# Attention scores as row tiles with each head on its own partition half, part of layer 2's output weights decoded inside layer 2, and a new order of work

## The chip, the cores and the metric

The kernel runs on one core of one Trainium2 chip. The metric is the device time of one execution in microseconds. Before the change three runs took 1127.84, 1130.23 and 1132.29 us; the median is 1130.23 us.

## The reference

The program is an attention layer followed by two dense layers. Inputs and results are float32.

```python
# attention: q, k, v are (4, 8, 576, 64); q and k get a rotary embedding first
scores = 1/sqrt(64) * q_rot @ k_rot.T          # per batch and head, 576 x 576
attn   = exp(scores - rowmax);  attn /= rowsum + 1e-9
x      = attn @ v                              # laid out as (2304, 512)
# layer 1: w_in (512, 2048), w_out (2048, 512)
h = x @ w_in;   g = h * clip(h + 3, 0, 6) / 6;   x = g @ w_out
# layer 2: same sizes, a has 4 coefficients and b has 2
h = x @ w_in
P = a0 + a1*h + a2*h^2 + a3*h^3
Q = 1 + |b0|*|h| + |b1|*h^2
out = (P / (Q + 1e-6)) @ w_out
```

The weights reach the core as 64-bit floats, so each weight has to be turned into float32 on the core ("decoded").

## The kernel before

**Precision.** Most products are split in two: a float32 number is scaled and written as a float16 head plus a float16 remainder ("hi" and "lo"), and a product is the sum hi*hi + hi*lo + lo*hi, accumulated in PSUM. Layer 2's second product uses a float32 form of matmul with the same three terms.

**Attention.** The work goes by pairs of heads: 4 batches with 4 pairs each. For one pair, `start_qk` (line 898) loads k and q into a tile `nat`. The 576 rows of a head lie as four groups of 128 rows and a tail of 64; the two heads share the fifth group, so the tile has NB = 9 groups of 128 rows for two heads. ScalarE takes a bound of the magnitudes (`bound`, line 749), a small matmul with ones adds it over the partitions (`total`, line 758), and VectorE makes a power-of-two scale of it (`pow2`, line 695). `prep_qk` (line 919) applies the rotation on VectorE (lines 934, 941, 944), writes hi (line 629, 631 or 635 by engine) and lo (line 954), side by side in 128 columns, and one DMA transpose on SyncE's queue brings them to `qkt`, in which the partitions are 64 hi dimensions and 64 lo dimensions. Two more transfers (line 964) write `k2`, the same keys with the two partition halves swapped.

`unit` (line 968) is one block of scores. A "full" unit has 128 query rows of each of the two heads (2 x 576 scores a row); a "small" unit has the tails, 64 rows of each head on the two halves of the output partitions. Every score is two matmuls over all 128 partitions (line 1002): one with `qkt` (hi*hi + lo*lo) and one with `k2` (hi*lo + lo*hi). There are 64 full units and 16 small ones. VectorE takes the row maximum (line 1006), ScalarE the exponential (line 1018), the result is split in hi and lo (lines 629 or 633, and 1026), transposed by DMA (line 1029, `pt`), multiplied with v on TensorE (line 1057), evicted (`xu`) and normalised (`norm`), and transposed by DMA again into `xt` (line 1097), which lies in the attention pool.

**Layer 1.** `layer1` (line 1123) takes 256 tokens at a time; nine blocks in all. For 16 slices of the hidden dimension it does the first product (line 1152), the activation on ScalarE and VectorE (lines 1159, 1161, 1165), then the second product (line 1181) and the write of the result to memory (`y1d`, line 1193). A ninth block collects the tails of the four batches.

**Weights.** `load_raw` (line 717) loads one 512 KB tile of 64-bit weights; `decode` (line 726) turns it into float32 with two ScalarE passes (lines 734, a Prelu, and 736) and one VectorE pass (line 739). Layer 1's 32 tiles are used from on-chip memory. For layer 2, `prep_w2` (line 822) decodes 32 tiles (16 of W_in, then 16 of W_out) while attention and layer 1 run and writes each to memory (`w2d`, line 828); in layer 2, `split_w2` (line 1296) reads them back through three buffers `w2s` (line 1298) and splits them.

**Layer 2.** Five blocks of 512 tokens (the last has 256), 16 steps each. A step is a first product (line 1380), thirteen passes on ScalarE and VectorE (lines 1388 to 1404) and a second product accumulated over the steps (line 1413). Layer 2's tiles lie in two pools: `p2` takes the space of the attention pool and opens when every operation on the attention pool is done (`to_left`, line 1265), `p2r` takes the space of layer 1.

**The order.** Nothing is issued where it stands in the code. `op` records each operation with the engines that may do it, its cost, its priority and its data dependencies, and `order` (line 452) walks through a model of the engines in time: whenever an engine is free it takes the ready operation with the smallest priority number. The result is a fixed order of instructions for each engine and queue. The priorities come from the position in the program (`at`, `at2`) plus offsets by tile name (`o_...`, and `z_...` for the first batch) in the table `PR`. A string such as `'AG'` in the table names the engines that may do an operation (A ScalarE, D VectorE, G GpSimd), the first one preferred; `pen` is added to the priority on the others. Nearly all transfers are issued by SyncE's queue, in order; a transfer that has to wait for a buffer or for data holds up those behind it.

Of the kernel before, what the change touches and what calls it, by code (L numbers as in the profile page):

```python
# [10 lines left out]
F32 = mybir.dt.float32  # L11
# [12 lines left out]
S = 576  # L24
D = 64
HP = 4
NB = 9
DM = 512
# [10 lines left out]
 'c01': 7.051,  # L39
 'e': 2,  # L40
 'e_ev': 'AD',
 'e_ev0': 'DA',
 'e_gh': 'G',
 'e_gh0': 'AD',
# [4 lines left out]
 'e_mx': 'AG',  # L49
 'e_mx0': 'A',  # L50
 'e_ob': 'A',
 'e_qk': 'AGD',
 'e_qk0': 'A',
# [6 lines left out]
 'e_v': 'GD',  # L60
 'e_v0': 'DA',
# [11 lines left out]
 'e_y': 'D',  # L73
# [6 lines left out]
 'l0q': 111.276,  # L80
 'l1o': 10.002,
 'l1p': -1.281,
 'l1r': 77.612,
 'lead': 12.176,
 'lead0': -2.288,
# [4 lines left out]
 'o_': -4.68,  # L90
 'o_ab': -119.56,
 'o_ac0': -215.72,
 'o_ac1': -584.53,
 'o_ac2': -339.1,
 'o_ac3': -294.85,
 'o_acc': -425.76,
 'o_bb': 473.96,
 'o_cf': 224.73,
 'o_d': 309.78,
 'o_down': -26.62,  # L100
 'o_downi': -228.51,
 'o_dv': 109.2,
 'o_e': -286.55,
 'o_f32': 34.2,
 'o_g2l': 57.65,
 'o_gh': 370.8,
 'o_gl': -30.13,
 'o_h': 2.51,
 'o_h2': -146.66,
 'o_half': -517.61,  # L110
 'o_hh': 10.41,
 'o_hr': -514.06,
 'o_hs': -4.18,
 'o_hx': 11.06,
 'o_ident': -545.53,
 'o_k2': 25.35,
 'o_lgh': 105.85,
 'o_lgl': -50.66,
 'o_lq': 85.0,
 'o_lr': -318.72,  # L120
 'o_ls': 103.57,
 'o_lt': -33.88,
 'o_mx': 10.42,
 'o_na': -356.99,
 'o_nat': 12.98,
 'o_ob': -14.69,
 'o_ones': -646.58,
 'o_p1': 325.81,
 'o_p16': 10.73,
 'o_p16h': 293.66,  # L130
 'o_p16l': -306.11,
 'o_pt': -5.34,
 'o_pth': -589.79,
 'o_ptl': 669.69,
 'o_pw': 229.41,
 'o_pwi': -37.76,
 'o_qal': -278.91,
 'o_qam': -211.74,
 'o_qb': -353.38,
 'o_qk16': 1213.36,  # L140
 'o_qkt': -39.84,
 'o_qpi': -16.04,
 'o_qps': 13.14,
 'o_qpv': -190.27,
 'o_r': 15.85,
 'o_r0': 729.05,
 'o_raw': 45.94,
 'o_ropea': 11.43,
 'o_ropeb': -325.11,
 'o_s': 8.48,  # L150
 'o_shift': 92.35,
 'o_so': 597.84,
 'o_t': -774.55,
 'o_t0': 231.84,
 'o_t1': 745.61,
 'o_tab': -1032.75,
 'o_u': -155.38,
 'o_v9': 22.39,
 'o_vam': -425.01,
 'o_vm4': -590.92,  # L160
 'o_vnat': 254.14,
 'o_vnat0': 5.77,
 'o_vnat1': -226.94,
 'o_vpi': -611.24,
 'o_vps': -339.75,
 'o_vpv': 145.01,
 'o_vqi': 128.34,
 'o_vqs': -100.16,
 'o_vqv': 238.1,
 'o_vv': -599.43,  # L170
 'o_w0_': -195.86,
 'o_w1_': -207.38,
 'o_w2_': 89.43,
# [45 lines left out]
 'q_w2s': 'Q',  # L219
# [102 lines left out]
 'z_vps': 988.81,
# [1197 lines left out]
```

## Time and profile before

| | before |
|---|---|
| median of three runs | 1130.23 us |
| profiled execution, its own time | 1126.76 us |
| its span, first to last instruction | 1125.0 us |
| TensorE busy | 978.0 us (87%) |
| VectorE busy | 923.3 us (82%) |
| ScalarE busy | 783.8 us (70%) |
| GpSimd busy | 100.3 us (9%) |
| moved by DMA | 142.28 MB |

Busy times are sums over the instructions of an engine. In the rows PE is TensorE, PEld its weight loads, DVE VectorE, ACT ScalarE, POOL GpSimd, SP SyncE; a "q" behind a name is the engine's queue. L1002 is line 1002 of the kernel. A matmul's bar includes the time it takes to drain, so bars of consecutive matmuls overlap, and the distance between their starts tells what each one occupies. An "idle" entry names what ended the wait.

### The profile page before, as it was taken

The numbers are of one execution on the slowest core, as the hardware profiler recorded it, in microseconds if no ns is written. First come the engines' busy times: TensorE is split into PE (matmuls) and PEld (weight loads), VectorE is DVE, ScalarE is ACT, GpSimd is POOL, SyncE is SP. The second block draws the span as 40 slices with busy tenths as digits, with TensorE's granted clock in tenths as the row PEclk, the third lists the DMA queues.
The fourth block names the chain that finished last, engine by engine and source line by source line (L and its number), as shares of the span: only waits on it lengthen the run. The fifth ranks groups of instructions, "written<-read, shape, count | busy, mean of one in ns | idle before, by whom it ended". The sixth has DMA issues, their size and how long they took to land.

```text
span 1125.0 us, 20071 instructions
## 1 busy us (share of the span) xinstructions
PE 978.0 (87%) x7702; PEld 733.6 (65%) x7702; DVE 923.3 (82%) x1571; ACT 783.8 (70%) x1401; POOL 100.3 (9%) x124
## 2 busy tenths in 40 slices
PE   1344588889889899999899999799999999999996
PEld 1223377777778778788788888466566566556674
DVE  4999989899888898889883525799898898898886
ACT  7878977687665666656763327778786776686785
POOL 0200021001122011401020100000000000000000
PEclk9975789999999999999999999999999999999999
DMA  7989994998999879897997324412010010010010
GB/s 244 244 203 238 235 205 110 197 177 166 207 195 175 165 144 201 174 219 166 205 193 163 129 95 137 135 50 59 33 38 1 20 38 1 1 38 1 1 38 20
DMA packets 280081, 142.28 MB, mean 126 GB/s; under 512 B 239664, under 2 KB 257072, under 8 KB 279984
## 3 DMA queue, kind: packets, MB, share of 16 engines
q1 hardware_dynamic: 277040, 135.72, 54.0%
q10 hardware_dynamic: 2944, 5.28, 2.0%
q8 instruction: 60, 0.98, 0.4%
q14 instruction: 37, 0.30, 0.1%
HBM read 61.26 MB, written 17.83 MB: 70 GB/s over the span
## 4 chain that ended last, share of the span: by engine, by line
DVE 27%; PE 22%; ACT 20%; DMA 14%; issue 6%; SPq 1%; POOL 0%; ACTq 0%; DVEq 0%
PE h L1152 8%; DMA pt<-p 8%; PE h L1181 7%; DVE lt L1394 3%; ACT lr L1397 3%; ACT ls L1389 3%; ACT lq L1388 3%; PE h L1057 3%; DVE lq L1392 2%; DVE lq L1399 2%; DVE lt L1402 2%; ACT lt L1390 2%; ACT lr L1398 2%; DVE lt L1395 2%; DVE lt L1400 2%
## 5 line engine op out<-in xcount | busy, mean ns | idle before, releaser
L1152 PE MATMUL h<-xt,w 128*128 128x256 f16 x1728 | 200.4, 276 | 5.9 <-ACT xu L629 2.2
L1413 PE MATMUL ac<-w,lgh 128*128 128x512 f32 x576 | 188.9, 409 | 6.5 <-ACT ob L629 4.2
L1152 PEld LDWEIGHTS <-w 128*128 128x128 f16 x1728 | 169.5, 99 | 28.6 <-issue 7.2
L1181 PE MATMUL h<-gh,w 128*128 128x256 f16 x1080 | 187.9, 273 | 0.0
L1181 PEld LDWEIGHTS <-w 128*128 128x128 f16 x1620 | 157.0, 98 | 17.9
L1380 PEld LDWEIGHTS <-w 128*128 128x128 f16 x960 | 90.1, 98 | 102.8 <-issue 20.8
L1181 PE MATMUL h<-gl,w 128*128 128x256 f16 x540 | 147.2, 273 | 0.0
L1413 PEld LDWEIGHTS ac<-w,lgh 128*128 128x128 f32 x576 | 106.2, 188 | 36.4 <-ACT lgh L1403 6.8
L1018 ACT ACTIVATE e<-s,mx,qal 128x576 f32<-128x576 f32 (+1 forms) x144 | 113.4, 832 | 23.7 <-DVE p L1026 11.4
L1413 PE MATMUL ac<-w,lgl 128*128 128x512 f32 x288 | 115.6, 401 | 2.6 <-DVE lgl L1404 1.9
L1057 PE MATMUL h<-v,pt 128*128 128x130 f16 (+3 forms) x1600 | 90.0, 214 | 31.9 <-DMA pt<-p 18.9
L1380 PE MATMUL hh<-x,w 128*128 128x512 f16 (+1 forms) x516 | 109.3, 363 | 4.7 <-ACT ls L1389 4.7
L1026 DVE TENSOR_TENSOR p<-e,p 128x1152 f16<-128x1152 f32 (+1 forms) x80 | 100.9, 1263 | 12.7 <-ACT p L629 11.9
L1057 PEld LDWEIGHTS <-pt 128*128 128x128 f16 (+1 forms) x1600 | 84.6, 104 | 39.6 <-DMA pt<-p 24.7
L1002 PEld LDWEIGHTS <-qkt 128*128 128x128 f16 (+1 forms) x704 | 52.6, 110 | 80.3 <-issue 41.2
L1006 DVE TENSOR_REDUCE mx<-s 128x2 f32<-128x1152 f32 (+1 forms) x80 | 98.8, 1241 | 0.5 <-PE s L1002 0.5
L1002 PE MATMUL s<-qkt 128*128 128x512 f16 (+3 forms) x352 | 70.2, 305 | 31.0 <-ACT e L1018 17.7
L1159 ACT ACTIVATE t<-h,half,d 128x512 f32<-128x512 f32 (+1 forms) x96 | 61.5, 667 | 46.2 <-PE h L1152 36.1
L1380 PE MATMUL hx<-x,w 128*128 128x512 f16 (+1 forms) x444 | 91.9, 356 | 1.3 <-DVE t L635 1.3
L736 ACT ACTIVATE raw<-raw,down 128x512 int32<-128x512 uint16 x64 | 48.5, 760 | 39.8 <-DMA raw<-in_moe_w_out_dram 25.7
L1400 DVE SCALAR_TENSOR_TENSOR lt<-lt,na,lr 128x512 f32<-128x512 f32 (+1 forms) x80 | 55.3, 694 | 18.5 <-ACT lr L1398 18.3
L1413 PEld LDWEIGHTS ac<-w,lgl 128*128 128x128 f32 x288 | 54.0, 188 | 24.3 <-DVE lgl L1404 13.4
(155 smaller groups left out, 1651.7 us busy)
## 6 DMA issues: line engine op xcount, KB each, us to landing
raw<-in_moe_w_in_dram SPq DMA_DIRECT2D x32, 512.0 KB, 4.9
raw<-in_moe_w_out_dram SPq DMA_DIRECT2D x32, 512.0 KB, 4.3
w2d<-f SPq DMA_DIRECT2D x32, 256.0 KB, 4.8
w2s<-w2d SPq DMA_DIRECT2D x32, 256.0 KB, 2.6
y1d<-t SPq DMA_DIRECT2D x18, 256.0 KB, 2.7
vnat<-in_v_dram SPq DMA_DIRECT2D x16, 256.0 KB, 3.4
nat<-in_k_dram SPq DMA_DIRECT2D x16, 256.0 KB, 4.0
nat<-in_q_dram SPq DMA_DIRECT2D x16, 256.0 KB, 3.4
```

The source lines that it names most:

```text
L736: op("A", c_act(512, 1) + 40, lambda e: act.activation(t()[:, :, 0], t().rearrange("p n two -> p (n two)").bitcast(U16).rearrange("p (n x) ...
L1002: pe.matmul(x[i][0], lhsT=x[i][1], rhs=x[i][2], start=(x[i][3] == 0), stop=(x[i][3] == 1))
L1006: op("D", c_dve(n), lambda e: vec.reduce_max(mx()[:, 0, 0:g], sv().rearrange("p (g n) -> p g n", g=g), axis=AX.X, negate=True), r=[s], w=[ ...
L1018: op("A", c_act(n // g, 2, False), lambda e, h=h: act.activation(et()[:, h * (n // g):(h + 1) * (n // g)], sv()[:, h * (n // g):(h + 1) * ...
L1026: op(EN("lo"), c_sub(n), lambda e: EL[e].tensor_tensor(ph()[:, n:2 * n], et()[:, 0:n], ph()[:, 0:n], ALU.subtract), r=es + [(ph, 0)], w=[( ...
L1057: pe.matmul(ob()[r0:r0 + m, o:o + k], lhsT=w, rhs=vv[:, 0:k], start=(z == 0 and j == 0), stop=(z == 1 and j == 4))
L1152: pe.matmul(hp()[:, o:o + NQ], lhsT=wt[kk]()[:, z, c:c + 128], rhs=x, start=(n == 0), stop=(n == 11))
L1159: act.activation(seg(t, c, n), seg(hp, c, n), AF.Relu, bias=half(), scale=x()[:, g:g + 1])
L1181: pe.matmul(yp()[:, o:o + NQ], lhsT=w[:, s_, m_ * 128:(m_ + 1) * 128], rhs=gt()[:, f], start=(f == 0 and z == 0), stop=(f == KF - 1 and z ...
L1380: pe.matmul(hp()[:, 0:n], lhsT=wi[kk]()[:, z, c:c + 128], rhs=xt()[:, kk, y, 0:n], start=(i == 0), stop=(i == 11))
L1400: op("D", l2_dve(n, 1), lambda e: vec.scalar_tensor_tensor(s(t), s(t), na()[:, 0:1], s(rr), ALU.add, ALU.mult), r=[rr, na], w=[t])
L1413: pe.matmul(accs[j][i]()[0:m], lhsT=gt()[:, x:x + m], rhs=wt(), start=(f == 0 and z == 0), stop=(f == KF - 1 and z == 2))
```

## The change

Keys and queries get the same layout as the values already have: `nat` becomes two standing tiles with five groups of 128 rows for each head (NS = 5), whose fifth group is zero on the other head's half of the partitions (zeroed once). The rotation works on 1280 instead of 1152 elements a partition, its last step is written to a new tile `rot` in two instructions, with the two heads side by side, and hi and lo become separate planes. After the transpose (20 blocks of 128 x 128 instead of 18) each head lies on its own half of the partitions, 64 dimensions each. The copy `k2` and its transfers go. A score is now three matmuls, hi*hi + hi*lo + lo*hi; in a full unit, head 0's are over partitions 0 to 63 and head 1's over 64 to 127, into different banks of PSUM, and the tail's keys of both heads are one full-height matmul, since the zeros separate the heads. A small unit uses full-height matmuls throughout.

Fifteen of the 16 tiles of layer 2's W_out are no longer decoded in `prep_w2`; `load_w2` loads and decodes them in layer 2 into tiles of their own in the pool `p2`, and `split_w2` takes them from there. The buffers `w2s` go from three to two.

The table `PR` gets new values nearly throughout: priorities, offsets and engine choices. The planner's costs of transfers go up by some 10%.

```diff
+ NS = 5
- 'e_ev': 'AD', 'e_mx': 'AG', 'e_qk': 'AGD', 'e_v': 'GD', 'e_y': 'D', 'q_w2s': 'Q', 'pen': -1.576
+ 'e_ev': 'A',  'e_mx': 'DA', 'e_qk': 'GD',  'e_v': 'G',  'e_y': 'AD', 'q_w2s': 'QA', 'pen': -82.267
...
+    ntt = [tl("attn", [128, 2, 2, NS, D], F32, f"nat{i}") for i in range(2)]
+    for i in range(2):
+        for h in range(2):
+            op("D", 155, lambda e, i=i, h=h: vec.memset(ntt[i]()[64 - 64 * h:128 - 64 * h, :, h, 4], 0.0), w=[(ntt[i], "0")])
...
-        op(en, cost, lambda e: EL[e].tensor_tensor(t(), t(), tb(), ALU.add), r=[(tb, 0), (tb, 1)], w=[(nat, 0), (nat, 1)])
+        rot = tl("attn", [128, 2, NS, 2, D], F32, "rot", 1)
+        for i in range(2):
+            op(en, {"D": c_dve(640), "G": c_pool(640)}, lambda e, i=i: EL[e].tensor_tensor(
+                rot()[:, i].rearrange("p j h d -> p h j d"), nat()[:, i], tb()[:, 2 * i:2 * i + 2], ALU.add),
+               r=[nat, (tb, 0), (tb, 1)], w=[(rot, i)])
...
-        for h in range(2):
-            op(PR["q_k2"], c_in(490, 730, 250, 1850), lambda e, h=h: DE[e].dma_start(
-                out=k2()[64 * h:64 * h + 64], in_=r()[64 - 64 * h:128 - 64 * h, 0]), r=[(r, 0)], w=[(k2, h)])
...
         def mm(e):
+            def kq(i, z, r0, r1):
+                return qk()[r0:r1, i, z].rearrange("p j e -> p (j e)")
+            if both:
+                todo = [[(h, a, b, c, x) for x in ((0, 0), (0, 1), (1, 0))]
+                        for h, a, b, c in ((0, 0, 512, 0), (1, 640, 1024, 0), (1, 1024, 1152, 384))]
+                for h, a, b, c, (y, z) in [x for u in zip(todo[0], todo[1]) for x in u] + todo[2]:
+                    pe.matmul(s()[:, a:b], lhsT=kq(1, y, 64 * h, 64 * h + 64)[:, cc * 128:cc * 128 + 128],
+                              rhs=kq(0, z, 64 * h, 64 * h + 64)[:, c:c + b - a], start=(y + z == 0), stop=(y == 1))
+                for y, z in ((0, 0), (0, 1), (1, 0)):
+                    pe.matmul(s()[:, 512:640], lhsT=kq(1, y, 0, 128)[:, cc * 128:cc * 128 + 128],
+                              rhs=kq(0, z, 0, 128)[:, 512:640], start=(y + z == 0), stop=(y == 1))
+            else:
+                for y, z in ((0, 0), (0, 1), (1, 0)):
+                    pe.matmul(s()[:, 0:512], lhsT=kq(1, y, 0, 128)[:, 512:640], rhs=kq(0, z, 0, 128)[:, 0:512],
+                              start=(y + z == 0), stop=(y == 1))
+                for i, (y, z, h) in enumerate([(y, z, h) for y, z in ((0, 0), (0, 1), (1, 0)) for h in range(2)]):
+                    kk = kq(0, z, 0, 128)[:, 512 + 64 * h:576 + 64 * h].unsqueeze(1).to_broadcast([128, 2, 64])
+                    pe.matmul(s()[:, 512:640], lhsT=kq(1, y, 0, 128)[:, 512:640], rhs=kk, start=i == 0, stop=i == 5)
...
-    for z in range(2 * KF):
+    for z in range(2 * KF - PR["wd"]):
         at(PR["w20"] + z * (PR["w21"] - PR["w20"]) / (2 * KF))
         prep_w2(z // KF, z % KF)
...
+    def load_w2(f):
+        raw = load_raw(w2o, False, f, True)
+        w2f[1, f] = tl("p2", [128, 512], F32, f"w2f{f}")
+        decode(raw, w2f[1, f])
...
-        t = tl("p2", [128, 512], F32, "w2s", 3)
+        if (wi, f) in w2f:
+            t = w2f[wi, f]
+        else:
+            t = tl("p2", [128, 512], F32, "w2s", 2)
...
+    for f in range(KF - PR["wd"], KF):
+        at2(PR["wd0"] + PR["wd1"] * f)
+        load_w2(f)
```

## Rows read from the trace of the kernel before

**Rows 1.** Busy time by stage (start:end us, length, busy us and instructions, clock, DMA)

```profile
0.00:150.00 150.00, 62.29 (x443) 42.81 (x444) 124.19 (x235) 123.82 (x246) 15.89 (x20) 0.81 0.93 231
150.00:605.00 455.00, 417.50 (x4516) 351.99 (x4514) 396.44 (x631) 304.10 (x510) 74.08 (x88) 0.98 0.91 180
605.00:697.00 92.00, 91.16 (x837) 81.63 (x835) 37.52 (x67) 38.26 (x79) 10.29 (x16) 1.00 0.39 117
697.00:812.00 115.00, 108.02 (x510) 66.32 (x508) 100.66 (x166) 91.21 (x158) 0.00 (x0) 0.99 0.27 81
812.00:1125.00 313.00, 299.06 (x1406) 190.82 (x1404) 264.54 (x475) 226.44 (x410) 0.00 (x0) 1.00 0.05 18
```

**Rows 2.** Chain of waits from 150 to 605 us, its shares by line

```profile
by line: DMA pt<-p 16.1%; PE h L1152 10.7%; PE h L1181 9.6%; PE h L1057 6.2%; issue 5.8%; DMA raw<-in_moe_w_in_dram 4.6%; PE s L1002 4.3%; DVE mx L1006 3.7%; DVE p L1026 3.6%; DMA qkt<-ropea 3.1%; DVE gl L1165 2.6%; DVE t L1161 2.5%; DMA vn
```

**Rows 3.** TensorE's waits from 0 to 150 us: us in total, times, longest

```profile
PE h L1057 <- DMA pt<-p: 8.8, 6, 2.4
PE s L1002 <- DMA qkt<-ropea: 8.2, 2, 6.3
PE s L1002 <- DMA k<-qkt: 5.7, 3, 3.1
```

**Rows 4.** The same from 150 to 605 us

```profile
PE h L1057 <- DMA pt<-p: 10.1, 8, 2.1
```

**Rows 5.** Timeline of TensorE, one full unit: start us, us, instruction, [idle before]

```profile
267.38 0.57 PE L1002 MATMUL s<-qkt 128*128 128x512 f16 x2
...
268.36 0.27 PE L1181 MATMUL h<-gh,w 128*128 128x256 f16 x1
```

**Rows 6.** Timeline of TensorE, two small units one after the other

```profile
426.99 0.41 PE L1002 MATMUL s<-qkt 128*64 128x512 f16 x2
427.23 0.38 PE L1002 MATMUL s<-k,qkt 128*64 128x512 f16 x2
...
427.57 0.39 PE L1002 MATMUL s<-qkt 128*64 128x512 f16 x2
427.79 0.38 PE L1002 MATMUL s<-k,qkt 128*64 128x512 f16 x2
```

**Rows 7.** DMA queues (packets, MB, share of 16 engines), and the key copies' issues

```profile
q1 hardware_dynamic: 277040, 135.72, 54.0%
q10 hardware_dynamic: 2944, 5.28, 2.0%
...
k<-qkt ACTq DMA_DIRECT2D x26, 144.0 KB, 4.1
```

**Rows 8.** Groups by line and shape, VectorE: count, busy us, mean ns, idle before

```profile
L934 DVE SCALAR_TENSOR_TENSOR ropea<-nat,tab 128x576 f32<-128x576 f32 x32 | 24.0, 765 | 7.3 <-DMA qkt<-ropea 5.4 <-DMA k<-qkt 1.0 <-DMA nat<-in_q_dram 0.9
L941 DVE TENSOR_TENSOR nat<-nat,tab 128x1152 f32<-128x1152 f32 x16 | 21.6, 1350 | 0.2
...
L633 DVE COPY xu<-h 128x260 f32<-128x260 f32 x20 | 8.5, 424 | 3.9 <-PE h L1057 3.9
```

**Rows 9.** The same view, the decode of one weight tile

```profile
L736 ACT ACTIVATE raw<-raw,down 128x512 int32<-128x512 uint16 x64 | 48.5, 760 | 39.8 <-DMA raw<-in_moe_w_out_dram 25.7 <-DMA raw<-in_moe_w_in_dram 13.9
...
L739 DVE SCALAR_TENSOR_TENSOR f<-f,raw 128x512 int32<-128x512 int32 x33 | 23.0, 696 | 17.5 <-ACT f L734 17.4
L734 ACT ACTIVATE f<-raw 128x512 f32<-128x512 f32 x33 | 22.1, 670 | 9.3 <-DMA w2d<-f 9.3
```

**Rows 10.** Busy time by stage of line 734 alone, one pass per decoded tile

```profile
150.00:605.00 455.00, 16.14 (x24) 0.98 0.91 180
605.00:697.00 92.00, 5.31 (x8) 1.00 0.39 117
```

**Rows 11.** Timelines of SyncE's queue, TensorE and ScalarE at the start of layer 2

```profile
696.38 12.61 SPq L1298 DMA_DIRECT2D w2s<-w2d  x7
...
717.26 6.83 PE L1380 MATMUL hh<-x,w 128*128 128x512 f16 x24 [4.68 <-ACT ls L1389]
717.81 1.28 ACT L1397 ACT_TABLE_LOAD   x1
```

More of the change, by code (lines that the diff above doesn't have):

```diff
@@ new lines @@
+ 'o_half': -103.62,
+ 'o_hh': 15.68,
+ 'o_hr': -395.49,
+ 'o_hs': -5.71,
+ 'o_hx': 15.09,
+ 'o_ident': -403.8,
+ 'o_k2': -142.58,
+ 'o_lgh': 70.04,
+ 'o_lgl': -581.99,
+ 'o_lq': 18.14,
+ 'o_lr': -123.91,
+ 'o_ls': 304.83,
+ 'o_lt': -372.33,
+ 'o_mx': 15.84,
+ 'o_na': -465.11,
+ 'o_nat': -305.94,
+ 'o_nat0': 45.34,
+ 'o_nat1': 129.69,
+ 'o_ob': -15.17,
+ 'o_ones': -634.81,
+ 'o_p1': 895.42,
+ 'o_p16': 13.11,
+ 'o_p16h': 132.86,
+ 'o_p16l': -385.03,
+ 'o_pt': 34.12,
+ 'o_pth': -413.89,
+ 'o_ptl': 495.44,
@@ new lines @@
+ 'o_pw': 35.35,
+ 'o_pwi': -257.48,
+ 'o_qal': -687.9,
+ 'o_qam': -212.59,
+ 'o_qb': -803.88,
+ 'o_qk16': 825.26,
+ 'o_qkt': -454.57,
+ 'o_qpi': -159.44,
+ 'o_qps': -5.98,
+ 'o_qpv': -319.4,
+ 'o_r': 17.77,
+ 'o_r0': 473.98,
+ 'o_raw': 216.86,
+ 'o_raw2': -192.45,
+ 'o_ropea': 10.38,
+ 'o_ropeb': 132.9,
+ 'o_rot': -6.37,
+ 'o_s': 8.87,
+ 'o_shift': 88.64,
+ 'o_so': 281.85,
+ 'o_t': -1177.27,
+ 'o_t0': -37.55,
+ 'o_t1': 600.66,
+ 'o_tab': -1216.31,
+ 'o_u': -110.88,
+ 'o_v9': 213.87,
+ 'o_vam': 41.33,
@@ new lines @@
+ 'z_ac1': -643.66,
+ 'z_ac2': 1566.75,
+ 'z_ac3': 154.26,
+ 'z_acc': 1154.56,
+ 'z_bb': -548.32,
+ 'z_cf': 171.79,
+ 'z_d': 891.23,
+ 'z_down': 1027.25,
+ 'z_downi': -311.78,
+ 'z_dv': 582.63,
+ 'z_e': -131.84,
+ 'z_f32': -840.49,
+ 'z_g2h': 234.36,
+ 'z_gh': -385.88,
+ 'z_gl': -27.84,
+ 'z_h': -1.68,
+ 'z_h2': -499.0,
+ 'z_half': -882.07,
+ 'z_hh': 83.8,
+ 'z_hr': -325.04,
+ 'z_hs': -449.06,
+ 'z_hx': 187.72,
+ 'z_ident': -50.9,
+ 'z_k2': -456.94,
+ 'z_lgh': 352.19,
+ 'z_lgl': -1350.85,
+ 'z_lq': 587.76,
@@ new lines @@
+ 'z_lr': -382.08,
+ 'z_ls': 262.72,
+ 'z_lt': -543.66,
+ 'z_mx': 438.55,
+ 'z_na': -508.55,
+ 'z_nat': -151.59,
+ 'z_nat0': -464.6,
+ 'z_nat1': 11.97,
+ 'z_ob': -16.05,
+ 'z_ones': -370.9,
+ 'z_p1': 72.62,
+ 'z_p16': -106.48,
+ 'z_p16h': 49.47,
+ 'z_p16l': -1221.72,
+ 'z_pt': -181.03,
+ 'z_pth': 1132.41,
+ 'z_ptl': -260.59,
+ 'z_pw': -557.88,
+ 'z_pwi': -464.29,
+ 'z_qal': 147.31,
+ 'z_qam': -366.26,
+ 'z_qb': -448.13,
+ 'z_qk16': 808.95,
+ 'z_qkt': -233.39,
+ 'z_qpi': -201.97,
+ 'z_qps': 130.7,
@@ new lines @@
+ 'z_qpv': -620.02,
+ 'z_r': -548.83,
+ 'z_r0': -1018.46,
+ 'z_raw': -866.63,
+ 'z_raw2': 143.28,
+ 'z_ropea': -255.31,
+ 'z_rot': -353.19,
+ 'z_s': 1228.73,
+ 'z_shift': 350.91,
+ 'z_so': -201.04,
+ 'z_t': 423.53,
+ 'z_t0': -713.56,
+ 'z_t1': 161.79,
+ 'z_tab': -74.19,
+ 'z_u': 167.92,
+ 'z_v9': 490.1,
+ 'z_vam': 91.27,
+ 'z_vm4': 16.87,
+ 'z_vnat': -734.01,
+ 'z_vnat0': 366.59,
+ 'z_vnat1': -1013.69,
+ 'z_vpi': -54.89,
+ 'z_vps': 1372.34,
+ 'z_vpv': 8.37,
+ 'z_vqi': 1169.35,
+ 'z_vqs': -327.62,
@@ L364, in cls @@
+ 'z_w2s': 639.84,
+ 'z_wam': 415.97,
+ 'z_wao': -175.34,
+ 'z_woi': -658.92,
+ 'z_wos': 415.81,
+ 'z_wov': -670.71,
+ 'z_wpi': -925.21,
+ 'z_wps': -5.8,
+ 'z_x2': 108.88,
+ 'z_x20': -549.67,
+ 'z_x21': -400.41,
+ 'z_x2pi': -689.57,
+ 'z_x2ps': 773.6,
+ 'z_x2pv': -247.55,
+ 'z_xf': 87.04,
+ 'z_xg': -121.04,
+ 'z_xh': -71.33,
+ 'z_xl': 180.15,
+ 'z_xn': -245.21,
+ 'z_xr': 199.09,
+ 'z_xt': 21.76,
+ 'z_xu': 67.96,
+ 'z_y0': 921.82,
+ 'z_y1': 469.29,
+ 'z_y1d': 84.78,
+ 'z_y1m': 173.14}
 def cls(nm):
@@ L1004, in unit @@
+        op("P", PR["sp"] if both else 850, mm, r=[qk], w=[s])
         g = 2 if both else 1
```

518 lines of the change are left out of this document (190 added, 328 removed).

## The prediction

> **What bounds the kernel now.** I read the busy table by stage first, then the chain of waits of the long middle stage, then what the tensor engine waits for, then single units. The table [rows 1] splits the span in five. From 0 to 150 us batch 0's attention starts while layer 1's weights are loaded and decoded: DMA 0.93 busy, VectorE and ScalarE 83% each, TensorE 62 of 150 us. From 150 to 605 the other batches' attention is mixed with layer 1's matmuls, and three resources are near full at once: DMA 0.91, TensorE 417.5 of 455 us, VectorE 396 of 455. From 605 to 697 TensorE finishes layer 1 almost alone (91 of 92 us). From 697 layer 2 runs, TensorE 94 to 96% busy, VectorE 85 to 88%. So the end is set by TensorE's work plus its idle time: 37.5 us between 150 and 605, 88 us before, 7 us in layer 2's first stretch. Whatever shortens attention without filling those gaps only lengthens the stretch at 605.
>
> The chain of waits of the middle stage [rows 2] gives the landing of the transposed probabilities (pt<-p) 16% of it, more than any other line; layer 1's two matmul lines follow with 11% and 10%. TensorE's own waits name the same transfers: 10.1 us for pt between 150 and 605 [rows 4]; in the first 150 us 8.8 us for pt, 8.2 us for the transposed keys and queries, and 5.7 us for the swapped copy of the keys [rows 3].
>
> **The change part by part.** All sums are against the profiled execution's own time, 1126.76 us (span 1125.0 and 1.8 around it), which lies 3.5 us under the median of the runs, 1130.23.
>
> *Scores.* One full unit now takes from 267.38 to 268.36 us, 0.98 us, for 2304 streamed columns [rows 5]. After, a unit streams 3x512 columns for head 0, 3x384 and 3x128 for head 1 on the other row half, and 3x128 full-height ones for the tail. If the halves run side by side without loss, that is 3x512+3x128 = 1920 columns, 0.98x1920/2304 = 0.82 us; if head 1's 384 columns start with head 0's 512 each time, the last 128s run partly alone: 2176 columns, 0.93 us; with no overlap at all 3456 columns, 1.47 us. No row tile is in this trace. The nearest rows are the small units [rows 6], which put two heads on two column halves: a pair of 512-column matmuls occupies 0.22 us (427.57 to 427.79), as long as one alone (0.98x512/2304), and the pair after the switch from the full array takes 0.24. So halves do overlap and a switch of shape costs about 0.02 us. I take 0.91 us: 64 x -0.07 = -4.5 us; ends -10 and +31. The small units lose what they had: from 426.99 to 427.57, 0.58 us, they go to 3x512+6x128 = 2304 full-height columns, 0.98 us: 16 x 0.40 = +6.4 us. Net for TensorE: +2 us (-4 to +38).
>
> The Trainium skill (TensorE: Matmul & The Clock Gate, "Part 3: Packing small matmuls") says that matmuls start and end strictly in program order whatever tile they sit on. By that rule head 1's last three pieces can't run under head 0's, the unit stays at 2304 columns and 0.98 us, and the net would be +6.4. The pairs in the rows have equal lengths, so this trace neither agrees nor disagrees.
>
> *No second copy of the keys.* 32 transfers of 144 KB go. With six y1 loads they make up the ACT queue's 5.28 MB, which take 2.0% of the 16 engines' span, 22.5 us [rows 7]; by bytes (4.72 MB in all, 6 of the 32 on the other queue) that is 20 us of DMA time. The 26 issues of ScalarE's queue go too. What they cover: in the first stage TensorE waits 5.7 us for this copy by name, and no new hop takes its place, since scores then start on the transpose itself. The transposes grow from 18 to 20 blocks of 32 KB, 32 blocks in all, 1.05 MB; at queue 1's average (607 us for 135.7 MB) that is +5 us. Zero padding and the larger rotation: VectorE's turn goes from 576 to 640 elements, 765 to about 830 ns (slope from the two rope rows, (1350-765)/576 = 1.02 ns an element [rows 8]). A pair has two turns, one product, a sum (now in two instructions) and two remainders: 8x64 elements more, 0.52 us, and one instruction more, by the fixed part of that line 765-576x1.02 = 0.18 us; 16 pairs: +11 us. Against it most of 20 evictions of 424 ns leave VectorE (8.5 us; only the first batches may still choose it). Net +3 (0 to +11) on VectorE, which lies beside DMA and TensorE in the middle stage; I count it at nothing there, and at all of it if VectorE becomes the bound.
>
> *15 tiles decoded later.* Each tile is a 512 KB load, two ScalarE passes (760 and 670 ns), one VectorE pass (696) [rows 9] and a 256 KB write. Of 32 such tiles of layer 2, 24 decodes (W_in of layer 2 first) run in 150-605 and 8 in 605-697 [rows 10]. With 17 left, and the quiet stretch at 605 still able to take 8, the middle stage keeps 9 to 17: 7 to 15 fewer. In 605-697, where nearly only such transfers move, 0.39x92 us moved 117 GB/s x 92 = 10.8 MB, 3.3 us a MB, so a tile's 0.79 MB cost 2.6 us: 18 to 39 us of DMA time, and 5 to 10 of VectorE, leave the middle stage.
>
> *What that is worth.* DMA work up to 605 falls by 20-5+(18 to 39) = 33 to 54 us of about 554 (0.93x150+0.91x455). If DMA alone bounded the stage it would shrink as much; if TensorE did, by nothing, and TensorE has 37.5 us to give. I take about half of these, -18 us (0 to -34), because the transfers lead the chain but name only 10 of the 37.5 us. In the first stage I take the copy's waits, 5.7, as -6 us (0 to -12, with part of the 8.2 and 8.8).
>
> *Layer 2's start.* The tiles' space is that of the attention pool, which is free only after layer 1's last first-product has read its input near that stretch's end, so almost none of the 15 can run in it. They land in 697-812, where ScalarE has 115-91.2 = 23.8 us idle and VectorE 14.3 [rows 1]; 15 tiles want 15x1.43 = 21.5 and 10.4. They fit on paper, at 97 to 98% on both, beside a TensorE that waits for both. Bounds 0 and +21; I take +6. The tiles read back from memory have two buffers instead of three: seven issues now take 12.61 us, 1.8 each [rows 11], and could take 2.7; the first sixteen are W_in, and TensorE already waits 4.7 us for ScalarE before its fourth product there. 0 to +14, I take +3. The 15 reads that are saved ride on an idle DMA and give nothing.
>
> *Engine choices and the new order.* Who does which small copy, and the order of all queues (SP's loads, transposes and writes among them), change throughout. I can't work a gain from rows out of that; 0, with +-15.
>
> Sum: +2 -18 -6 +6 +3 = -13, about 1114 for an execution like the profiled one and 1117 against the median; I give 1116.
>
> **The rivals.** (1) *Relief that doesn't convert.* TensorE and VectorE, not DMA, hold the middle stage; for it: they are 92% and 87% busy, and 27 of TensorE's 37.5 idle us are not put down to pt; against it: the chain [rows 2]. Then +2 -6 +9, some 1128 to 1135. (2) *The other side: layer 2 starts late.* Place: 697-812; ScalarE's 21.5 us stand in front of the steps that TensorE waits for, and the W_in chain runs on two buffers. It decides as soon as the decode of a W_out tile lands after its step, and a step follows every 5.6 us (313 us for the last 56, rows 1). Price 21+9, attention -10, scores +2: +22, about 1149. For it: VectorE and ScalarE 88% and 79% busy there; against it: the tiles are needed one by one over the whole first block. (3) *DMA is the bound.* Nearly all of the 37.5 us go, layer 2 hides the rest: -34 -6 +2 +2, about 1091. (4) *Row halves don't overlap:* TensorE +38 in a stage with 37.5 idle, less the gains and with layer 2's 9: about 1150; the column halves speak against it. (5) *Table switches.* ScalarE loads a function table once at layer 2's first reciprocal root, 1.28 us [rows 11]; the decode's Prelu now falls behind it. If each tile had to switch and switch back, 30 x 1.28 = 38 us on an engine with 24 idle: about 1145. The code uses Square, Identity and Copy on both sides of that load and the line has the one load, which speaks against it; no row shows Prelu behind it. The Trainium skill (ScalarE activation tables: per-element evaluation and per-set limits, "What a function is on this engine") puts functions of different sets one load of 1283 ns apart, and the row's 1.28 us agrees; it doesn't say which set holds Prelu.
>
> **How the numbers follow.** Forecast 0.47, (1) 0.17, (2) 0.14, (3) 0.15, (4) 0.05, (5) 0.02. A measurement of this kernel tells 0.5%, 5.6 us, from no change. Faster: 0.42 of the forecast and (3), 0.57. Same: 0.05 of the forecast, 0.12 of (1), 0.17. Slower: 0.05 of (1), (2), (4), (5), 0.26. Range: from 1088, just under (3), to 1150, which takes in most of (2).
>
> **What would show it.** Right: full units near 0.9 us and small ones near 0.98; no waits for a key copy; DMA share of the middle stage near 0.85, and TensorE's idle time there near 20 us; layer 1 ending some 20 us earlier; layer 2's first stretch a little over 115 us, later blocks unchanged at 16x5.6 = 89. Wrong: layer 1 ending at 697 as before with TensorE's gaps now behind VectorE or ScalarE; layer 2's first stretch over 125 us; row halves one after another; table loads between decodes.

## The result and the profile after

| | before | after |
|---|---|---|
| median | 1131.12 us (4 runs) | 1095.95 us (1092.97 to 1098.43, 4 runs) |
| ratio of the runs, 95% interval | | 0.970 [0.968, 0.973] |
| profiled execution, its own time | 1126.76 us | 1092.97 us |
| its span | 1125.0 us | 1090.9 us |
| TensorE, VectorE, ScalarE busy | 978.0, 923.3, 783.8 us | 967.9, 930.0, 797.5 us |
| moved by DMA | 142.28 MB | 130.55 MB |

The kernel is 35 us faster; 1116 was forecast, so the direction was right and the size too small. Both profiled executions are their kernel's quickest, 3 to 4 us below the medians, so the two spans can be set against each other: -34.1 us.

Stage boundaries moved, so each kernel is cut at its own: the first matmul of layer 1, the last product with v, and the last second product of layer 1. Columns: stretch, length, busy us of TensorE, its weight loads, VectorE, ScalarE and GpSimd, granted clock, DMA share, GB/s. First the kernel before:

```profile
0.00:148.70 148.70, 60.99 (x431) 41.65 (x432) 122.89 (x228) 122.78 (x244) 15.89 (x20) 0.80 0.93 232
148.70:600.40 451.70, 414.20 (x4486) 349.06 (x4484) 394.79 (x632) 303.42 (x508) 73.46 (x87) 0.98 0.91 181
600.40:708.60 108.20, 107.28 (x962) 93.51 (x958) 44.78 (x79) 47.31 (x97) 10.91 (x17) 1.00 0.41 128
708.60:1125.00 416.40, 395.55 (x1832) 249.35 (x1832) 360.89 (x635) 310.31 (x553) 0.00 (x0) 0.99 0.10 30
```

The same of the kernel after:

```profile
0.00:146.60 146.60, 60.72 (x501) 46.83 (x502) 129.51 (x245) 120.17 (x242) 36.37 (x26) 0.70 0.96 232
146.60:568.00 421.40, 409.30 (x4611) 350.79 (x4608) 392.31 (x631) 301.57 (x513) 70.74 (x61) 1.00 0.87 172
568.00:672.40 104.40, 103.62 (x953) 92.62 (x951) 35.52 (x66) 45.28 (x96) 0.00 (x0) 1.00 0.24 77
672.40:1090.90 418.50, 394.23 (x1856) 254.08 (x1854) 372.70 (x649) 330.46 (x588) 0.00 (x0) 0.98 0.12 38
```

The whole gain lies between the first and the last matmul of layer 1: 559.9 us became 525.8. TensorE's idle time in the second row went from 37.5 to 12.1 us. The first stage gave 2.1 us, layer 2 took 2.1. TensorE's busy time in rows two and three fell by 8.6 us although the scores cost 3.8 more (below); of this the clock in the second row, 0.98 of the full 2.4 GHz before and 1.00 after, is some 8 us of 414 (an estimate from these rows).

TensorE's waits in the first stage (us in total, times, longest). Besides [rows 3] the list before has:

```profile
PE h L765 <- ACT junk L754: 35.1, 13, 7.1
PE h L765 <- DVE ropea L934: 13.8, 1, 13.8
PE s L1002 <- ACT e L1018: 12.2, 6, 2.8
```

After:

```profile
PE h L813 <- ACT junk L802: 35.8, 9, 15.0
PE s L1037 <- ACT e L1064: 15.0, 7, 5.4
PE h L1103 <- DMA pt<-p: 10.6, 5, 4.1
PE s L1037 <- DMA qkt<-ropea: 9.5, 4, 4.4
```

And from 146.6 to 568 us, against [rows 4]:

```profile
PE h L1198 <- ACT xu L672: 1.8, 2, 1.0
...
PE h L1198 <- DVE t L1207: 1.4, 3, 0.9
PE h L1103 <- DMA pt<-p: 1.2, 2, 0.7
```

The key copy's wait is gone from the first stage, but the waits for the transposes stayed (8.8 to 10.6 and 8.2 to 9.5 us), and so did those for ScalarE (35.1 to 35.8 and 12.2 to 15.0). The 13.8 us for VectorE went, but three other waits of about 5 us each came, so the stage hardly got shorter. In the middle the wait for pt fell from 10.1 to 1.2 us, and nothing took its place. The chain of waits of that stretch agrees; [rows 2] began with pt at 16.1%:

```profile
by line: PE h L1227 22.6%; PE h L1198 20.2%; PE h L1103 10.6%; PE s L1037 6.0%; DMA pt<-p 6.0%; PE s L1040 2.1%; DMA w2d<-f 1.5%; PE s L1044 1.2%; ACT e L1064 1.1%; issue 1.0%; ACT t L1205 0.8%; DVE p L1072 0.8%; PE s L1048 0.6%; DVE mx L10
```

The queues, against [rows 7]; no key copies are left:

```profile
q1 hardware_dynamic: 275904, 127.16, 52.4%
q10 hardware_dynamic: 1296, 2.10, 0.6%
```

A full unit and a small one on TensorE's timeline, against [rows 5, 6]:

```profile
401.62 0.83 PE L1037 MATMUL s<-qkt 64*128 64x512 f16 x9
402.38 0.34 PE L1040 MATMUL s<-qkt 128*128 128x128 f16 x3
402.56 0.27 PE L1227 MATMUL h<-gh,w 128*128 128x256 f16 x1
...
288.43 0.81 PE L1044 MATMUL s<-qkt 128*128 128x512 f16 x3
289.07 0.50 PE L1048 MATMUL s<-qkt 128*128 128x128 f16 x6
289.41 0.38 PE L1044 MATMUL s<-qkt 128*128 128x512 f16 x1
```

From 401.62 to 402.56 a full unit occupies 0.94 us (0.98 before), a small one 0.98 (0.58): 64 x -0.04 + 16 x 0.40 = +3.8 us. The last matmul on a row half of this unit, and the first of the tail that follows it:

```profile
402.23 0.22 PE L1037 MATMUL s<-qkt 64*128 64x128 f16 x1
402.38 0.28 PE L1040 MATMUL s<-qkt 128*128 128x128 f16 x2
```

A 128-column matmul occupies about 0.06 us (the tail's three take 402.38 to 402.56), and head 0's last 512 columns, begun at 402.06, need the 0.22 us of [rows 6]. So some 0.09 us between the halves and the tail stand empty.

Line 782 is the decode's Prelu; its passes by stage, against [rows 10] (24 and 8):

```profile
146.60:568.00 421.40, 11.35 (x17) 1.00 0.87 172
568.00:672.40 104.40, 2.01 (x3) 1.00 0.24 77
672.40:785.00 112.60, 8.04 (x12) 0.95 0.29 94
```

All 17 early tiles still lie in the middle stretch, three of the late ones in the quiet third one, twelve in layer 2. Layer 2 cut at the first eviction of its output, before:

```profile
708.60:814.50 105.90, 99.00 (x439) 59.63 (x440) 98.46 (x164) 84.95 (x146) 0.00 (x0) 0.98 0.22 64
814.50:1125.00 310.50, 296.56 (x1395) 189.72 (x1393) 262.43 (x471) 225.37 (x409) 0.00 (x0) 1.00 0.05 18
```

and after:

```profile
672.40:798.70 126.30, 109.16 (x476) 63.59 (x474) 115.50 (x188) 110.50 (x190) 0.00 (x0) 0.96 0.26 84
798.70:1090.90 292.20, 285.07 (x1380) 190.49 (x1380) 257.21 (x463) 219.97 (x399) 0.00 (x0) 0.99 0.06 19
```

TensorE's two longest waits in that first stretch after:

```profile
PE hx L1436 <- ACT w L1357: 6.7, 3, 4.9
PE hh L1436 <- DVE lt L1451: 5.3, 1, 5.3
```

ScalarE's timeline there (start, us) has the one table load that answers to [rows 11], and seven of the late Prelus lie behind it (697.8 to 754.1 us):

```profile
691.69 1.28 ACT L1453 ACT_TABLE_LOAD   x1
...
L782 ACT ACTIVATE w2f<-raw x7: 646/666/673, 697.8 to 754.1; 128x512 f32<-128x512 f32 x7
```

The first stretch got 20 us longer and the rest 18 shorter: TensorE waits there for ScalarE's splits and passes, 10 us more of its busy time lies in the first (476 matmul records against 439, at a clock of 0.96 against 0.98), and its idle time went from 6.9 to 17.1 there and from 13.9 to 7.1 in the rest.

### The profile page after: what moved, and what is told of

Same layout as the page of the kernel before. It is cut to its first block, busy times and chain, and to the rows that moved or that the text cites. A ratio compares the mean times of both kernels' runs of the same rounds, so it can differ in the third digit from the quotient of the medians.

```text
span 1090.9 us, 20357 instructions
## 1 busy us (share of the span) xinstructions
PE 967.9 (89%) x7910; PEld 744.3 (68%) x7910; DVE 930.0 (85%) x1591; ACT 797.5 (73%) x1438; POOL 107.1 (10%) x87
## 2 busy tenths in 40 slices
DMA packets 277296, 130.55 MB, mean 120 GB/s; under 512 B 242768, under 2 KB 260304, under 8 KB 277200
## 3 DMA queue, kind: packets, MB, share of 16 engines
q8 instruction: 62, 1.02, 0.4%
## 4 chain that ended last, share of the span: by engine, by line
PE 61%; ACT 7%; DVE 6%; DMA 3%; issue 1%; SPq 0%; ACTq 0%; DVEq 0%
PE h L1227 14%; PE ac L1469 14%; PE h L1198 12%; PE hh L1436 6%; PE hx L1436 6%; PE h L1103 4%; PE s L1037 2%; DMA pt<-p 2%; ACT lq L1444 1%; PE s L1040 1%; ACT lt L1446 1%; DVE lq L1455 1%; DVE lt L1450 1%; DMA w2d<-f 1%; DVE lgl L1460 1%
## 5 line engine op out<-in xcount | busy, mean ns | idle before, releaser
L1198 PE MATMUL h<-xt,w 128*128 128x256 f16 x1728 | 197.4, 274 | 6.4 <-ACT t L672 2.3
L1469 PE MATMUL ac<-w,lgl 128*128 128x512 f32 x288 | 112.9, 392 | 0.0
L1436 PE MATMUL hx<-x,w 128*128 128x512 f16 (+1 forms) x444 | 94.4, 362 | 6.7 <-ACT w L1357 6.7
L1207 DVE SCALAR_TENSOR_TENSOR t<-t,h 128x512 f32<-128x512 f32 x72 | 49.1, 683 | 56.6 <-ACT t L1205 56.3
L1037 PE MATMUL s<-qkt 64*128 64x512 f16 (+2 forms) x576 | 61.5, 344 | 24.5 <-ACT e L1064 15.0
L1037 PEld LDWEIGHTS <-qkt 64*128 64x128 f16 x576 | 36.4, 101 | 45.9 <-issue 21.1
L1453 ACT ACTIVATE lr<-lq,qb 128x512 f32<-128x512 f32 (+1 forms) x80 | 53.6, 677 | 14.8 <-DVE lq L1448 14.1
L1469 PEld LDWEIGHTS ac<-w,lgl 128*128 128x128 f32 x288 | 54.0, 188 | 12.2
```

What stands on the lines that cost most here:

```text
L1037: pe.matmul(s()[:, a:b], lhsT=kq(1, y, 64 * h, 64 * h + 64)[:, cc * 128:cc * 128 + 128], rhs=kq(0, z, 64 * h, 64 * h + 64)[:, c:c + b - a] ...
L1198: pe.matmul(hp()[:, o:o + NQ], lhsT=wt[kk]()[:, z, c:c + 128], rhs=x, start=(n == 0), stop=(n == 11))
L1207: op("D", c_dve(2 * NQ), lambda e, t=t, hp=hp: vec.scalar_tensor_tensor(t(), t(), two(-15), hp()[:, 0:2 * NQ], ALU.min, ALU.mult), r=[hp], ...
L1436: pe.matmul(hp()[:, 0:n], lhsT=wi[kk]()[:, z, c:c + 128], rhs=xt()[:, kk, y, 0:n], start=(i == 0), stop=(i == 11))
L1453: op("A", l2_act(n, 1), lambda e: act.activation(s(rr), s(q), AF.Abs_reciprocal_sqrt, bias=qb()), r=[q, qb], w=[rr])
L1469: pe.matmul(accs[j][i]()[0:m], lhsT=gt()[:, x:x + m], rhs=wt(), start=(f == 0 and z == 0), stop=(f == KF - 1 and z == 2))
```

## The experiments

The theories: **T**, the transfers that go (key copies, 15 tiles) were what TensorE's gaps came from; **W**, it was the wait for the copy, not its transfer; **O**, the gain comes from the new order or the engine choices by themselves. In the expectations theory 1 is T and theory 2 is O. Ratios are against the kernel before, timed in the same sets of runs (1129 to 1132 us), with a 95% interval. In the first two groups and in the row-half trial TensorE's matmuls keep their order unless said otherwise.

**The key copies.** b_nok2 is the kernel before without them: nothing is issued in their place, and line 1002 reads `qkt` twice, so the cross terms of the scores are left out.

```diff
-            op(PR["q_k2"], ..., lambda e, h=h: DE[e].dma_start(out=k2()..., in_=r()...), r=[(r, 0)], w=[(k2, h)])
+            op(PR["q_k2"], ..., lambda e, h=h: None, r=[(r, 0)], w=[(k2, h)])
```

> The kernel before, same order, but the 32 copies of the keys into k2 aren't issued and both matmuls of a score read qkt (so the scores are not the reference's; the amount of work on TensorE is). If transfers hold the attention phase (theory 1): the 20 us of DMA time and the 5.7 us of named waits go, 1115 to 1122 us. If the gain of the change came from the new order (theory 2): 1126 to 1131, since SyncE's and the engines' order is what sets the pace.

Measured 1115.87 us, 0.987 [0.986, 0.989]: -14 us. b_k2nowait issues the copies and reads `qkt` twice, so nothing waits for them:

> The kernel before, same order, with all 32 key copies still issued at their places, but both matmuls of a score read qkt, so nothing waits for a copy (the scores are not the reference's). Leaving the copies out altogether gave -14 us. If that was the transfer time: 1126 to 1131 us here. If it was the wait for the copy: 1115 to 1120. With both parts, in between.

Measured 1131.33 us, 1.000 [0.998, 1.002]. At the old order the wait was worth nothing and the copies themselves 14 us; W falls. The 14 us are the transfers together with their issues: 26 of the 32 copies are issued by ScalarE, 0.47 us each, and no run parts the two. a_k2load puts copies of nearly that size back into the kernel after, one pair for each pair of heads on ScalarE's queue, with no reader:

> The changed kernel, same order, with two dummy copies of the keys of 140 KB a pair put back on ScalarE's queue behind each pair's first exponential; nothing waits for them. Only the DMA time (about 20 us) and ScalarE's issues come back. Theory 1: 1105 to 1112 us. Theory 2: 1096 to 1100.

Measured 1102.19 us, 0.975 [0.973, 0.977], 6 us above the kernel after, between the two ranges expected: at the new order the copies cost less than half of the 14 us. The middle stretch of b_nok2, cut as above:

```profile
148.30:589.40 441.10, 410.40 (x4488) 347.91 (x4484) 396.19 (x632) 302.62 (x508) 72.32 (x87) 0.99 0.89 177
```

of b_k2nowait:

```profile
153.00:605.10 452.10, 413.86 (x4484) 349.18 (x4483) 394.59 (x625) 302.78 (x507) 71.48 (x87) 0.99 0.92 180
```

and of a_k2load:

```profile
148.80:575.70 426.90, 408.96 (x4612) 350.28 (x4610) 392.74 (x636) 301.11 (x513) 71.66 (x61) 1.00 0.90 179
```

TensorE idles 30.7 us without the copies, 38.2 with copies that nobody waits for, and 17.9 in the kernel after with dummy copies (12.1 without).

**The fifteen tiles.** b_no15 neither loads, decodes nor writes 15 tiles of layer 2's W_out (layer 2 reads one tile 16 times); b_nok2_no15 does both.

```diff
+        if wi == 1 and f > 0:
+            for o in pl.ops[n0:]:
+                o.fn = lambda e: None
```

> The kernel before, same order, but tiles 1 to 15 of layer 2's W_out are neither loaded nor decoded nor written (layer 2 reads tile 0 in their place). 15 of 32 tiles' transfers go, most from 500 us on, where DMA is over 0.9 busy. Theory 1: 1118 to 1124 us. Theory 2: 1127 to 1131, since most of the 15 fall near or in the quiet stretch.

> Both left out at the old order. Theory 1: the whole of the relief, 1105 to 1115 us, the middle stage's idle time of TensorE from 37 to under 25 us. Theory 2: 1122 to 1130, idle time still over 30 us.

Measured 1126.22 us, 0.997 [0.995, 0.999], and 1111.55 us, 0.984 [0.982, 0.986]: -4 us, between the two ranges expected, and -18 us. The middle stretch of the second has 28.2 us of idle time left, at a DMA share of 0.84:

```profile
148.70:584.80 436.10, 407.92 (x4488) 345.69 (x4484) 391.96 (x626) 293.39 (x494) 74.23 (x87) 1.00 0.84 166
```

The other way round, a_wd0 is the kernel after with all 32 tiles decoded early (`'wd': 0`; compared place by place in the two traces, 9% of TensorE's matmuls differ), and a_wd0_s3 has three read-back buffers besides:

> The changed kernel with all 32 tiles decoded early again (the order is worked out anew with the same priorities; two read-back buffers stay). If decoding 15 tiles in layer 2 pays: 1100 to 1108 us. If it is paid back in layer 2's first block: 1093 to 1099.

> The changed kernel with all 32 tiles decoded early, as the 1089 us version, and three read-back buffers in layer 2, for which there is room again. If the W_in chain on two buffers holds the start of layer 2: 1083 to 1087 us, layer 2's start with less idle time of TensorE. If not: 1087 to 1092.

Measured 1089.15 us, 0.963 [0.961, 0.966], and 1089.04 us, 0.963 [0.960, 0.966]. Late decoding costs 7 us here, which neither expected range allowed, and the third buffer is worth nothing. a_wd0 beats both kernels. Its rows from the middle stretch on, and the decode's Prelus in the first two of them:

```profile
146.30:592.90 446.60, 431.01 (x4804) 369.56 (x4802) 400.35 (x642) 308.96 (x530) 68.45 (x56) 1.00 0.88 174
592.90:681.40 88.50, 87.93 (x784) 76.16 (x782) 42.04 (x75) 53.23 (x111) 0.92 (x1) 1.00 0.52 155
681.40:1089.00 407.60, 388.93 (x1832) 251.54 (x1830) 362.53 (x634) 315.21 (x561) 0.00 (x0) 0.99 0.11 33
...
146.30:592.90 446.60, 14.04 (x21) 1.00 0.88 174
592.90:681.40 88.50, 7.34 (x11) 1.00 0.52 155
```

Layer 1 ends 9.0 us later than in the kernel after (681.4 against 672.4), and layer 2 is 10.9 us shorter (407.6 against 418.5). That makes 1.9 us between two profiled executions of which one lies above its median and the other below; the medians differ by 6.8. The middle stretch idles 15.6 us, 3.5 more, with 21 early tiles in place of 17; the other 11 run in the quiet stretch, where the kernel after decoded three. So the transfers of all 32 tiles fit in before layer 2 with TensorE hardly waiting more.

**Row halves.** a_seq issues head 0's three 512-column matmuls and then head 1's six, instead of alternating.

```diff
-                for h, a, b, c, (y, z) in [x for u in zip(todo[0], todo[1]) for x in u] + todo[2]:
+                for h, a, b, c, (y, z) in todo[0] + todo[1] + todo[2]:
```

> The changed kernel, same order of operations, but inside a full unit head 0's three 512-column matmuls are issued first, then head 1's six, instead of in turn. If row tiles overlap only where they are issued side by side, a unit grows from 0.94 to about 1.3 us and 64 units cost 15 to 25 us: 1108 to 1120. If a later matmul on the free row half starts early whatever stands before it: 0.9 to 1.0 us, 1094 to 1099.

Measured 1094.83 us, 0.969 [0.966, 0.971], the same as the kernel after. One of its units, line 1037 in two windows of 0.1 us from 265.1 us on (ns min/median/max, first and last start, forms running):

```profile
L1037 PE MATMUL s<-qkt x2: 332/360/387, 265.1 to 265.1; 64*128 64x512 f16 x1, 64*128 64x384 f16 x1
...
L1037 PE MATMUL s<-qkt x3: 323/332/387, 265.1 to 265.3; 64*128 64x384 f16 x2, 64*128 64x512 f16 x1
```

Head 1's first matmul, fourth in the queue, starts beside the first of all, and its second starts before head 0's second. Here each row half works through its own matmuls.

**Engine choices.** b_mxact moves 20 small scalings of the row maximum from GpSimd to ScalarE in the kernel before; a_oldeng is the kernel after with the old engine and queue letters and the old `pen`.

> The kernel before, same order, with the 20 small scalings of the row maximum that ran on GpSimd (808 ns each, and ScalarE's exponential waited 9.9 us for five of them) issued on ScalarE at the same place in the order. The changed kernel has none on GpSimd. If this engine choice is a visible part of the new order's gain: 1122 to 1127 us. If the waits are off the path: 1128 to 1132.

> The changed kernel with its new priorities, but the old engine and queue choices and the old penalty for a second choice; the order is worked out anew. The whole old table gave 1165 us. If the engine choices carry the gain of the new table: 1110 to 1150. If the priorities do: 1095 to 1106.

Measured 1131.06 us, 1.000 [0.998, 1.002], and 1118.51 us, 0.989 [0.986, 0.992]: the scalings' engine is worth nothing, the letters 23 us against the kernel after. But the letters also steer the planner, and 45% of TensorE's matmuls, place by place, differ from the kernel after, so the second number has to be read beside the random orders below.

**The order.** a_oldorder is the new structure with the old table of priorities and letters; b_neworder is the old structure with the new table.

> The changed kernel's structure (row tiles, no key copy, 15 tiles decoded in layer 2) with the old table of priorities and engine choices; only the settings that the old table lacks keep their new values. Theory 1 (the gain is the relief of the transfers): 1100 to 1112 us. Theory 2 (half of the gain or more is the new order): 1115 to 1140, since the old priorities don't fit the new operations.

> The old structure with the new table of priorities and engine choices, all 32 tiles decoded early, the key copy issued first by SyncE's queue. Theory 1: 1122 to 1135 us, as before. Theory 2: 1105 to 1118; the order alone carries some 17 us.

Measured 1165.27 us, 1.032 [1.029, 1.035], and 1142.95 us, 1.012 [1.009, 1.014]. Each table is bad on the other structure, worse than either theory expected, so O in its plain form, a better table that would help either kernel, falls. The planner's transfer costs alone, new ones in the kernel before (b_newcost) and old ones in the kernel after (a_oldcost):

> The kernel before with the planner's costs of transfers as in the kernel after (some 10% higher), its priorities, engine choices and instructions unchanged; only the order of issue can change. If the better cost model carries the order's share of the gain (16 to 20 us), this comes to 1110 to 1120 us. If that share is a table of priorities that suits one structure and one set of costs, the old table suffers from the new costs: 1130 to 1150, equal to before or slower. If the costs don't matter, 1127 to 1133.

> The kernel after with the planner's old costs of transfers, everything else unchanged. If the cost model carries the order's share, 1112 to 1120 us (16 to 20 over the kernel after's 1096). If the table was fitted to everything around it, also above 1096, but with no size of its own: 1100 to 1130. If the costs don't matter, 1094 to 1098.

Measured 1143.57 us, 1.011 [1.007, 1.014], and 1145.49 us, 1.013 [1.010, 1.015]: 12 and 50 us worse than the kernel each comes from. So the costs don't help the old table. The 50 us, above every range expected, are more than twice what a random draw costs (below): the new table leans on the new costs. What remained was whether the new table is simply better fitted than the old one. a_jit, a_jit2, b_jit and b_jit2 move the `o_` and `z_` offsets at random by up to one step (1.0); place by place, 44 to 52% of TensorE's matmuls differ from the fitted kernel's. The line of a_jit for the PSUM tiles `h`, as one of its 265:

```diff
- 'o_h': 1.85,
+ 'o_h': 2.65,
```

> The kernel after with every priority offset by tile name moved by a random amount of up to one step of the table either way; no instruction, engine choice or buffer differs, only the order. If the order's gain lies in something that can be named and is robust (for instance loads ahead of transposes), the time stays at 1093 to 1101 us. If it is the fit of the whole table to this structure, a random small shift loses a good part of it: 1106 to 1130.

> The kernel before with every priority offset moved by a random amount of up to one step either way, as in the same trial on the kernel after. If the old table is as closely fitted to its structure, 1140 to 1165 us; if small shifts do nothing, 1126 to 1135; faster than 1120 would mean that the old table had room left, and that the gain of the new order needed no change of structure.

> The kernel after with a second random draw of the same size (every offset by tile name moved by up to one step either way). The first draw gave 1117, 21 us above the kernel after. If that is what any disturbance of the table costs, 1110 to 1125; if the first draw was an accident, under 1103 or over 1130.

> The kernel before with a second random draw of the same size. The first gave 1148, 16 us above the kernel before. If both tables stand equally far above their neighbours, 1140 to 1155, and the structures differ by some 25 to 35 us at equal disturbance, so that the search of priorities is no source of the gain. If this draw comes near 1125, the structures differ by 10 or less, and the gain beyond the key copies' transfers is the new table's own.

| | fitted | first draw | second draw |
|---|---|---|---|
| kernel before | 1131 | 1147.87, 1.014 [1.012, 1.017] | 1152.06, 1.019 [1.016, 1.022] |
| kernel after | 1096 | 1117.00, 0.987 [0.985, 0.989] | 1117.57, 0.988 [0.985, 0.992] |
| difference, us | 35.2 | 30.9 | 34.5 |

Both tables are worth some 20 us against a neighbour (17 and 21 before, 21 and 22 after), and the two kernels differ by as much disturbed as fitted. So the gain does not lie in the fine fit of these offsets. The draws leave alone in each kernel its structure, its engine letters and `pen`, its planner's costs and the rest of its table; which of these the 31 to 34 us belong to, they don't tell. What a bad order costs is seen in the middle stretch of b_jit2:

```profile
142.40:623.40 481.00, 428.23 (x4554) 357.09 (x4553) 411.38 (x654) 315.06 (x525) 76.36 (x91) 0.96 0.89 179
```

of a_oldcost:

```profile
144.90:618.30 473.40, 431.01 (x4699) 366.31 (x4697) 397.57 (x625) 305.93 (x524) 64.49 (x60) 0.96 0.79 153
```

and of a_jit2:

```profile
146.70:583.60 436.90, 412.39 (x4613) 352.20 (x4611) 389.32 (x628) 306.83 (x525) 63.92 (x57) 0.99 0.84 167
```

TensorE idles 52.8, 42.4 and 24.5 us. The second has the transfers of the kernel after, at a DMA share of 0.79, and idles more than the kernel before: fewer transfers do not close the gaps by themselves.

## Why the prediction was right in direction and too small

**Scores: held.** +2 was forecast, +3.8 measured. Full units took 0.94 us against 0.91. The model with 2176 columns (0.93) is met in its number, which is luck: by it head 1's last pieces run partly alone, but the trace has the halves side by side nearly without loss, as in the model with 1920 columns (0.82), and 0.09 us empty before the tail, where the forecast read 0.02 for a switch of shape from the column halves. The rival in which the halves don't overlap (4) is out. The rule of the Trainium skill (TensorE: Matmul & The Clock Gate, "Part 3: Packing small matmuls"), by which matmuls start and end in program order whatever their tile, would have given 0.98; the full unit's row and a_seq's starts differ from it, and the measurement decides.

**No key copies: the size held, the cover did not.** In the first stage the copy's 5.7 us of named waits were forecast as -6; the stage gave 2.1, and the waits for ScalarE and the two transposes are no shorter than before. b_k2nowait shows the same more sharply: a wait with a name in the profile was worth nothing. The copies, some 20 us of transfer time by the forecast's sum, and their issues were worth 14 us at the old order and 6 at the new one.

**Fifteen tiles: too high.** The forecast let 7 to 15 decodes leave the middle stage. It was seven, since the planner moved none of the 17 remaining into the quiet stretch, and b_no15 prices the removal of all 15 at 4 us at the old order. The other half, that the late tiles make layer 2's start longer, was right in place: +9 forecast, and the first stretch of layer 2 has 10 us more idle time. Of that the later blocks gave 7 back, which the forecast's "later blocks unchanged" excluded; the length of layer 2 grew by 2, and why the later blocks gained isn't shown. a_wd0 says that at the new order this part of the change costs 7 us in the end. No table was switched for the late Prelus: seven of the twelve run after the load at 691.69, and no other load follows it, so rival (5) is out. The page named there (of the Trainium skill: ScalarE activation tables: per-element evaluation and per-set limits, "What a function is on this engine") gives 1283 ns for a load, and the row shows 1.28 us again.

**The middle stage, -18, and the step that failed.** With copies and tiles taken out at the old order, -18 us were measured (b_nok2_no15), against -18 forecast for the middle stretch and -6 for the first stage, which stayed as long as it was (148.7 us). So the middle's term held at the old order. The step that failed is the last: "Engine choices and the new order: 0, with ±15". From 1111.55 to 1095.95 are another 15.6 us, and the kernel after pays 3.8 us for the scores and up to 7 for the late tiles on top, so by prices of the old order the term was some -19 to -26. By prices of the new order it was larger: there the copies are worth 6 us and the late tiles cost 7, which nearly cancel and leave some -40 for the term (an estimate; it takes the parts as additive). Either way it lies beyond its bounds.

The term was treated as independent of the relief, and the runs show that it is not: the copies cost 14 us under one order and 6 under the other, and a table made for one structure loses on the other. Taking out a transfer while the order stays fixed therefore shows only what that order lets through. So T is shown for 18 us at the old order (transfers together with their issues and the tiles' decodes) and not for the rest: the kernel after idles for 12.1 us, a_oldcost with the same transfers for 42.4, and a_wd0 with 15 tiles' transfers back before layer 2 for 15.6. What earns the remainder stays open: the row tiles' structure, the engine letters, the planner's new costs, and the table made with them have not been parted. No run fits a new table to the old structure, with the new costs or without its copies, and undoing the letters alone (a_oldeng) costs about what a random draw costs.

**The rivals.** Relief that doesn't convert (1) is out, and so is a late layer 2 (2): its place was right, its 30 us were not. Rival (3) came nearest: it let nearly all of the 37.5 idle us go and layer 2 hide the rest, and arrived at 1091. Two thirds of the idle time went, and layer 2 did hide its share. It is near in its number; that DMA was the bound isn't shown, and a_oldcost, with 42.4 us of idle time at a DMA share of 0.79, speaks against it.

## What to carry to other kernels

A named wait is no price: here taking away the wait for a copy gave nothing, and taking away the copy gave 14 us. A price found at one fixed order need not hold at another: the same copies cost 6 us at the new one. Where a planner's table has been fitted to a kernel, undoing one part of a change also undoes the fit; disturb both versions equally at random, and compare those, but remember that this prices all that the draws leave alone together. Work moved to a later stage because a resource is full in the earlier one should be tried in both places: here it was 7 us cheaper to leave the tiles in the earlier one.

## What the runs showed of the hardware

Matmuls on the two row halves of the array did not keep their issue order between them: with head 1's six issued behind head 0's three, both halves started together and the unit took 0.94 us, as in the kernel after (265.12 to 266.06). Behind the halves some 0.09 us passed before the first full-height matmul (402.23 and 402.38 above).

Longer gaps in TensorE's work went with a lower clock. In the middle stretches with 42 to 53 us of idle time the granted clock was 0.96, in those with 37.5 and 38.2 us 0.98 and 0.99, and in the kernel after, with 12.1, it was 1.00. Of the two levels, 1.2 and 2.4 GHz, the slower stretches had the lower one for part of the time. No run holds the gaps and changes the clock alone, so what it adds to a gap isn't shown by itself. One slice of 50 us before:

```profile
200.00:250.00 50.00, 43.79 (x453) 36.23 (x452) 44.93 (x74) 39.68 (x70) 0.41 (x1) 0.97 0.94 190
```

and two after:

```profile
200.00:250.00 50.00, 47.72 (x544) 40.59 (x542) 49.24 (x79) 42.39 (x72) 6.06 (x6) 1.00 0.81 167
250.00:300.00 50.00, 48.88 (x569) 41.78 (x568) 45.71 (x74) 38.71 (x67) 0.00 (x0) 1.00 1.02 190
```

In both slices after TensorE was busier than before, once at a lower DMA share (0.81 against 0.94) and once at a higher one (1.02): the share of busy DMA alone does not tell how long TensorE waits.
